# Hand-placed loads and casts for the first eight pairs of heads, decay terms stored in two parts, and a new spread of MLP groups over three batches

## The chip, the cores and the metric

The kernel runs on one core of one Trainium2 chip. The metric is device time in microseconds (us), lower is better. The kernel before was timed seven times; the median is 383.22 us.

## The reference, cut to what matters

There are 8 batches of 8 heads, 576 positions of 64 values each. Attention is causal and has a decay: with `cum` the running sum of `max(s, 0)` of a head, the score of query i and key j has `cum[j] - cum[i]` added. Its output, 4608 rows of 512 values (the heads of a batch side by side), goes through two layers with a hard-swish between them.

```python
scores = scale * q @ k.T + (cum[None, :] - cum[:, None])   # causal, cum = cumsum(max(s, 0))
attn   = exp(scores - max); attn = attn / sum(attn)
x      = attn @ v                     # -> (4608, 512), heads of a batch side by side
h      = x @ w_in                     # 512 -> 2048
out    = (h * clip(h + 3, 0, 6) / 6) @ w_out               # 2048 -> 512
```

## The kernel before, in words

**Heads go in pairs.** There are 32 pairs, four to a batch. For each pair, SP (the engine that only issues DMAs) loads q and k (`load_qk`, L136 to L144, two DMAs of 288 KB into `qkf`, three buffers) and v (`load_v`, L146 to L157, three DMAs into `v_f`, three slots). GpSimd (POOL) casts q and k to 16 bits (`cast_qk`, L165 to L168); v is cast on VectorE (DVE) for pairs 1 to 4 and on POOL otherwise (`cast_v`, L226 to L229). Slots of `v_f`, `v_h` and `qkT` are taken by pair number modulo 3, so a load into a slot waits until the pair three before it has given it back.

**Transposes.** For pairs 0 to 9, TensorE (PE) transposes the nine tiles of a pair in two groups of five and four (`transpose_group`, L242 to L256), and DVE copies each group into q and k rows of `qkT`, two copies per group. From pair 10 on, the DMA transposes (`transpose_dma`, L219).

**Decay.** The running sum, times 8, is split into three 16-bit terms (`kaug`, L110 to L117) and its negative into one (`qaug`, L460). They are extra rows 64 to 67 of the transposed k and q, beside rows of ones and rows of the coarse causal mask (`mask_rows`, L125), so that the scores' matmul adds them. Pair 0 gets its rows directly from SBUF, by four short DMAs on SP and four on ScalarE's queue (L461 to L468). For pairs 1 to 9, all 64 heads are first stored to a scratch in DRAM by two DMAs on SP (L469 and L472), and each pair loads its rows from there by two (`load_aug`, L159 to L163). From pair 10 on, `decay_columns` and `copy_columns` (L175 to L209) have made them columns of the block that the DMA transposes.

**Scores and attention.** A head's scores come in four banks (`scores_bank`, L272 to L319): one or two matmuls, an exponential on ScalarE (ACT), a triangular mask on POOL. `attend` (L320 to L350) multiplies by v with 15 matmuls; after the second head of a pair DVE takes the reciprocal of the row sums and multiplies. `x_transpose` (L356 to L377) turns the result into the input of the MLP, on PE (with a copy on DVE) or by DMA.

**MLP.** Nine blocks of 512 rows. A group of the first layer (`m1`, L403 to L420) is four matmuls, a relu on ACT and a gate on DVE; there are 16 to a block. A group of the second (`m2`, L421 to L445) is four matmuls, and four groups make one output tile of 128 rows, scaled on DVE and stored by SP. The two halves of w_in and the four quarters of w_out are loaded and cast by DMAs that POOL issues (`load_w_in`, `load_w_out`).

**Order.** Nothing is reordered by a scheduler: each engine runs its instructions in the order in which the program lists them, and waits where data or a buffer is missing.[...] `att_tasks` (from L482) lists the tasks of a pair: scores of the first head, the first transpose group of the *next* pair, the second attend of the *previous* pair, scores of the second head, casts for the next pairs, the second transpose group, `x_transpose` of the previous pair, then the first attend. Pairs 0 to 3 and the scores of pair 4 run alone. Then `weave` (L546) spreads the attention tasks of a batch evenly, by costs written beside each task, among the groups of the MLP: 24 groups with batch 1, 24 with batch 2, 32 with each of batches 3 to 7; 80 groups are left after the last pair.

PSUM tiles come from rings by tag: `M` (two, for layer 1 and early transposes), `S` (three, for scores, later transposes and the decay), `O` (one, of two banks), and `Y` (one, for layer 2).

Of the kernel before, what the change touches and what calls it, by code (L numbers as in the profile page):

```python
# [16 lines left out]
def kernel(  # L17
# [27 lines left out]
    PTD = 10  # L45
# [24 lines left out]
    )  # L70
    kaug_dram = nc.dram_tensor("kaug_scratch", (3, NH * SEQ), F16, kind="Internal").ap()
    qaug_dram = nc.dram_tensor("qaug_scratch", (1, NH * SEQ), F16, kind="Internal").ap()

# [34 lines left out]
    )  # L108
    kaug = work.tile([NH, 3, SEQ], F16, tag="s3", bufs=1)
    qaug = work.tile([NH, SEQ], F16, tag="s4", bufs=1)  # L110
    r1 = work.tile([NH, SEQ], F32, tag="s0", bufs=1)
# [6 lines left out]

    nc.gpsimd.memset(warm, 0.0)
    nc.gpsimd.memset(kT[:, :, W2:W2 + 64], 0.0)  # L120
# [14 lines left out]

    def load_qk(p, eng):  # L136
        b, h0 = (2 * p) // H, (2 * p) % H
        t = work.tile([128, NTR, 2, D], F32, tag="qkf", bufs=3, name=f"qkf{p}")
        for i, src in enumerate((q, k)):
            rows = src[b, h0:h0 + 2].rearrange("h s d -> (h s) d")  # L140
            eng.dma_start(
                out=t[:, :, i, :], in_=rows.rearrange("(t p) d -> p t d", p=128)
            )
        qk_f[p] = t  # L144
# [14 lines left out]
    def load_aug(p, eng):  # L159
        sl = p % NS  # L160
        c0 = p * W2
        eng.dma_start(out=kT[64:67, sl, 0:W2], in_=kaug_dram[:, c0:c0 + W2])
        eng.dma_start(out=qT[67:68, sl, 0:W2], in_=qaug_dram[:, c0:c0 + W2])  # L163

# [61 lines left out]
    def cast_v(p):  # L226
        sl = p % NS
        copy = nc.vector.tensor_copy if p in (1, 2, 3, 4) else nc.gpsimd.tensor_copy
        copy(out=v_h[:, sl, :, :, 0:D], in_=v_f[:, sl])  # L229
# [12 lines left out]
    def transpose_group(p, g):  # L242
        t0, t1 = ((0, 5), (5, 9))[g]
        n = (t1 - t0) * 128
        pT = half_bank(p < 5)
        src = qk_h[p]
        for t in range(t0, t1):
            c = (t - t0) * 128
            transpose_tile(pT[:, c:c + 128], src[:, t, :, :], t == t0, t == t1 - 1)
        sl = p % NS  # L250
        c0 = t0 * 128
        for dst, r0 in ((qT, 0), (kT, 64)):
            nc.vector.tensor_copy(out=dst[0:64, sl, c0:c0 + n], in_=pT[r0:r0 + 64, 0:n])  # L253
        if g == 1:
            qk_h.pop(p)
# [147 lines left out]
    def m1(n, f):  # L403
        if f == 0:
            gT[n] = work.tile([128, NF, 512], F16, tag="gT", bufs=2, name=f"gT{n}")
        ph = bank()
        for kc in range(KC):
# [13 lines left out]
    def m2(n, t4, part):  # L421
        if part == 0:

            if (n, t4) in ((0, 1), (8, 1), (8, 3)):
                pouts[n, t4] = bank()
            else:
                pouts[n, t4] = psum.tile([128, 512], F32, tag="Y", name=f"po{n}_{t4}")
# [27 lines left out]
    load_qk(0, nc.sync)  # L455
    load_v(0, nc.sync)
    load_qk(1, nc.sync)
# [7 lines left out]
    for hh in range(2):  # L465
        c0, c1 = hh * SEQ, (hh + 1) * SEQ
        nc.sync.dma_start(out=kT[65:66, 0, c0:c1], in_=kaug[hh:hh + 1, 1, :])
        nc.scalar.dma_start(out=kT[66:67, 0, c0:c1], in_=kaug[hh:hh + 1, 2, :])  # L468
    nc.sync.dma_start(  # L469
        out=kaug_dram.rearrange("r (h t) -> h r t", h=NH), in_=kaug  # L470
    )
    nc.sync.dma_start(out=qaug_dram.rearrange("r (h t) -> h (r t)", h=NH), in_=qaug)  # L472
    mask_rows(1, nc.scalar.copy)
    load_v(1, nc.sync)
    load_aug(1, nc.sync)
    load_qk(2, nc.sync)
    load_v(2, nc.sync)

    weights_at = {1: [(load_w_in, 0)], 2: [(load_w_in, 1)]}
    pairs_at = {0: [3], 1: [4], 2: [], 3: [5], 4: [6], 5: [7, 8]}  # L480

    def att_tasks(p):  # L482


        more = p + 1 < NP

        def loads():
            if p + 2 < PTD:
                load_aug(p + 2, nc.sync)
            if p == 5:  # L490
                load_columns()
            for m in pairs_at.get(p, [p + 3] if p + 3 < NP else []):
                load_qk(m, nc.sync)
                load_v(m, nc.sync)
            if 4 < p < PTD - 1:
                cast_qk(p + 1)

        def casts():
            if more:
                cast_v(p + 1)  # L500
            if p + 2 <= 4:
                cast_qk(p + 2)
            if PTD <= p + 2 < NP:
                cast_columns(p + 2)
                transpose_dma(p + 2)
            for load, c in weights_at.get(p, []):
                load(c)

        def scores(hd):
            return [(lambda bi=bi: scores_bank(hd, bi), 400) for bi in range(4)]  # L510

        tr = [[], []]
        if p + 1 < min(NP, PTD):
            tr = [[(lambda: transpose_group(p + 1, 0), 640)],
                  [(lambda: transpose_group(p + 1, 1), 512)]]
        here = tr if p != 4 else [[], []]
        late = [(lambda: attend(2 * p - 1), 1200)] if p > 0 else []
        back = [(lambda: x_transpose(p - 1), 0 if by_dma(p - 1) else 640)] if p > 0 else []
        a = [(loads, 0)]
        if p <= PXD:  # L520
            a += scores(2 * p) + here[0] + late
            a += scores(2 * p + 1) + [(casts, 0)] + here[1] + back
        else:
            s0, s1 = scores(2 * p), scores(2 * p + 1)
            a = late + (back + a if by_dma(p - 1) else a + s0[:2] + back)
            a += (s0 if by_dma(p - 1) else s0[2:]) + here[0]
            a += s1 + [(casts, 0)] + here[1]
        if p == 6:
            a += [(decay_columns, 640)]
        if p == 7:  # L530
            a += [(copy_columns, 0)]
        c = [(lambda: attend(2 * p), 1200)]
        if p == 4:
            c += [(lambda: cast_qk(p + 1), 0)] + tr[0] + tr[1]
        return a, c

    att_of = [[]]
    for p in range(NP):
        a, c = att_tasks(p)
        att_of[-1] += a  # L540
        if p % 4 == 0 and p > 0:
            att_of.append([])
# [28 lines left out]
    def merged(a, b, rounds):  # L571
# [10 lines left out]
        return out_  # L582

    keep_warm(18)
    cast_qk(0)
    transpose_group(0, 0)
    transpose_group(0, 1)
    mask_rows(2, nc.vector.tensor_copy)
    cast_v(0)
    cast_qk(1)  # L590
    keep_warm(12)
    for task, _ in att_of[0]:
        task()

    first = [(task, 0.0 if f < 4 else 0.7) for f, (task, _) in enumerate(m1_tasks(0))]
    for c, f in enumerate((0, 2, 5, 8)):
        task, w = first[f]
        first[f] = ((lambda task=task, c=c: (task(), load_w_out(c))), w)  # L600
    m2_0 = m2_tasks(0)
    weave(att_of[1], first + m2_0[:8])
    weave(att_of[2], merged(m1_tasks(1), m2_0[8:], 2))
    for n in range(2, NBLK):
        weave(
            att_of[n + 1] if n + 1 < B else [],
            merged(m1_tasks(n), m2_tasks(n - 1), 4),
            0.85 if n + 1 == B - 1 else 1.0,
        )
    for task, _ in m2_tasks(NBLK - 1):  # L610
        task()

# [29 lines left out]
```

## Time and profile before

| what | value |
|---|---|
| median of 7 runs | 383.22 us (378.83 to 384.9) |
| the profiled execution | 384.71 us |
| its span in the profile | 383.0 us |
| mean granted clock of PE | 0.966 |
| busy: PE, ACT, DVE, POOL | 358.2, 210.3, 190.6, 146.0 us |
| DMA | 59.38 MB, 155 GB/s over the span |

The profile divides the span into 40 slices. In the rows of section 2, each digit is the busy share of a slice in tenths, in the row PEclk the clock that PE was granted, in the row DMA the mean busy share of 16 DMA engines. A busy PE can be at half clock, so that the two rows belong together. The busy share of DMA can exceed one, as packets overlap. The lists of waits give what an engine waited for, and the chain of waits follows the end of the program back. Lines such as L408 are lines of the kernel before.

### The profile page before, as it was taken

The numbers are of one execution on the slowest core, as the hardware profiler recorded it, in microseconds if no ns is written. First come the engines' busy times: TensorE is split into PE (matmuls) and PEld (weight loads), VectorE is DVE, ScalarE is ACT, GpSimd is POOL, SyncE is SP. The second block draws the span as 40 slices with busy tenths as digits, with TensorE's granted clock in tenths as the row PEclk, the third lists the DMA queues.
The fourth block names the chain that finished last, engine by engine and source line by source line (L and its number), as shares of the span: only waits on it lengthen the run. The fifth ranks groups of instructions, "written<-read, shape, count | busy, mean of one in ns | idle before, by whom it ended". The sixth has DMA issues, their size and how long they took to land.

```text
span 383.0 us, 7609 instructions
## 1 busy us (share of the span) xinstructions
PE 358.2 (94%) x2780; PEld 222.5 (58%) x2780; DVE 190.6 (50%) x329; ACT 210.3 (55%) x406; POOL 146.0 (38%) x375
## 2 busy tenths in 40 slices
PE   7775886899999999999999999999999999999995
PEld 2464454556666666666666666666666655555542
DVE  5544476656545454544454445444544454454531
ACT  4735556334777666666666666666666533443310
POOL 4465353426555545355535554544443200000000
PEclk9969599889999999999999999999999999999999
DMA  8699799926899999999997999889944101001012
GB/s 175 137 202 197 162 216 213 209 59 149 175 224 189 219 207 193 232 190 203 219 227 160 206 200 231 181 190 225 187 109 107 47 27 56 27 39 45 27 61 78
DMA packets 184621, 59.38 MB, mean 155 GB/s; under 512 B 177828, under 2 KB 178212, under 8 KB 184584
## 3 DMA queue, kind: packets, MB, share of 16 engines
q1 hardware_dynamic: 182536, 54.52, 66.9%
q0 software_dynamic: 1632, 4.19, 5.8%
q8 instruction: 22, 0.36, 0.4%
q10 hardware_dynamic: 416, 0.19, 0.2%
q14 instruction: 15, 0.12, 0.1%
HBM read 37.41 MB, written 9.73 MB: 123 GB/s over the span
## 4 chain that ended last, share of the span: by engine, by line
PE 82%; DMA 9%; DVE 3%; ACT 2%; issue 1%; SPq 1%; POOL 1%; POOLq 0%; ACTq 0%; DVEq 0%
PE bank L408 31%; PE po L430 30%; PE S L282 10%; PE O L331 7%; DMA qkf<-in_k_dram 5%; DMA v_f<-in_v_dram 3%; PE bank L430 3%; ACT Pm L290 2%; DMA s_sb<-in_s_dram 1%; PE pT L369 1%; DVE qkT L253 1%; PE bank L450 1%; POOL t L167 1%; DVE kaug L115 0%; PE pT L238 0%
## 5 line engine op out<-in xcount | busy, mean ns | idle before, releaser
L416 ACT ACTIVATE trl<-bank,bias 128x512 f32<-128x512 f32 x144 | 99.4, 690 | 114.8 <-PE bank L408 113.8
L417 DVE SCALAR_TENSOR_TENSOR gT<-trl,bank 128x512 f16<-128x512 f32 x144 | 99.0, 687 | 123.3 <-ACT trl L416 123.3
L408 PE MATMUL bank<-xT,w_in 128*128 128x512 f16 x576 | 150.0, 387 | 0.6 <-DVE gT L417 0.6
L290 ACT ACTIVATE Pm<-S 128x384 f16<-128x384 f32 (+2 forms) x256 | 116.2, 505 | 34.1 <-PE S L282 32.6
L430 PE MATMUL po<-w_out_sb,gT 128*128 128x512 f16 x528 | 131.8, 381 | 0.0
L295 POOL TENSOR_SCALAR_AFFINE_SELECT Pm<-Pm 128x128 f16<-128x128 f16 (+2 forms) x256 | 78.6, 310 | 138.6 <-ACT Pm L290 129.5
L408 PEld LDWEIGHTS <-w_in 128*128 128x128 f16 x576 | 77.7, 146 | 32.1 <-issue 3.7
L430 PEld LDWEIGHTS <-gT 128*128 128x128 f16 x576 | 53.4, 98 | 51.7 <-issue 0.5
L282 PE MATMUL S<-qkT 128*128 128x320 f16 (+4 forms) x448 | 71.4, 269 | 6.0 <-DMA qkT<-kaug_scratch 2.4
L282 PEld LDWEIGHTS <-qkT 128*128 128x128 f16 x448 | 42.2, 101 | 34.6 <-DMA qkT<-kaug_scratch 2.5
L331 PEld LDWEIGHTS <-Pm 128*128 128x128 f16 x960 | 40.2, 100 | 11.8 <-POOL Pm L295 0.4
L331 PE MATMUL O<-v_h,Pm 128*128 128x65 f16 x960 | 42.8, 197 | 0.2 <-POOL Pm L295 0.2
L343 DVE TENSOR_TENSOR xs<-O,r 128x640 f16<-128x640 f32 x32 | 26.4, 824 | 1.1
L213 POOL CAST xb<-qkf 128x1152 f16<-128x1152 f32 x22 | 25.2, 1147 | 0.0
L439 DVE TENSOR_SCALAR osb<-po 128x512 f32<-128x512 f32 x33 | 22.6, 684 | 5.0 <-PE po L430 5.0
L229 POOL CAST v_h<-v_f 128x640 f16<-128x640 f32 x28 | 20.6, 736 | 2.8 <-DVE gT L417 2.8
L341 DVE RECIPROCAL r<-O 128x10 f32<-128x10 f32 x32 | 7.0, 220 | 25.7 <-PE O L331 25.5
L167 POOL CAST t<-qkf 128x1152 f16<-128x1152 f32 x10 | 11.9, 1187 | 13.6 <-DMA qkf<-in_k_dram 13.6
L238 PEld LDWEIGHTS <-t 128*128 128x128 f16 x90 | 6.6, 101 | 13.9 <-POOL t L167 9.9
L253 DVE COPY qkT<-pTm 64x640 f16<-64x640 f16 (+1 forms) x20 | 9.1, 454 | 8.3 <-PE pTm L238 8.0
L253 DVE COPY qkT<-pT 64x640 f16<-64x640 f16 (+1 forms) x20 | 9.0, 452 | 6.1 <-PE pT L238 6.0
L430 PE MATMUL bank<-w_out_sb,gT 128*128 128x512 f16 x48 | 11.3, 379 | 0.0
(40 smaller groups left out, 80.5 us busy)
## 6 DMA issues: line engine op xcount, KB each, us to landing
qkf<-in_q_dram SPq DMA_DIRECT2D x32, 288.0 KB, 3.6
qkf<-in_k_dram SPq DMA_DIRECT2D x32, 288.0 KB, 4.3
out_dram<-osb SPq DMA_DIRECT2D x36, 256.0 KB, 2.0
v_f<-in_v_dram SPq DMA_DIRECT2D x64, 128.0 KB, 3.9
w_in<-in_moe_w_in_dram POOLq DMA_DIRECT2D x2, 1024.0 KB, 11.7
w_out_sb<-in_moe_w_out_dram POOLq DMA_DIRECT2D x4, 512.0 KB, 8.4
v_f<-in_v_dram SPq DMA_DIRECT2D x32, 32.0 KB, 7.4
qkT<-xb SPq DMA_TRANSPOSE x22, 5.0
```

The lines of the kernel that those rows point to most:

```text
L213: nc.gpsimd.tensor_copy(out=x.rearrange("p (i t) c -> p t i c", i=2)[:, :, :, 0:D], in_=qk_f.pop(p))
L253: nc.vector.tensor_copy(out=dst[0:64, sl, c0:c0 + n], in_=pT[r0:r0 + 64, 0:n])
L282: nc.tensor.matmul(out=S[:, c:c + hi - lo], lhsT=kT[:, sl, off + 128 * kt:off + 128 * (kt + 1)], rhs=qT[:, sl, off + lo:off + hi], start=( ...
L290: nc.scalar.activation(out=P[:, p0:p0 + n], in_=S[:, 0:n], func=AF.Exp, scale=0.125, bias=0.0)
L295: nc.gpsimd.affine_select(out=view, in_=view, pattern=pattern, compare_op=ALU.is_ge, fill=0.0, base=0, channel_multiplier=-1,)
L331: nc.tensor.matmul(out=O[:, hh, qt * VW:qt * VW + D + 1], lhsT=P[:, c:c + 128], rhs=v_h[:, sl, hh, kt, 0:D + 1], start=(qt == 0), stop=(qt ...
L343: nc.vector.tensor_tensor(out=xs.rearrange("p t h d -> p h t d"), in0=Ov[:, :, :, 0:D], in1=r.to_broadcast([128, 2, 5, D]), op=ALU.mult,)
L408: nc.tensor.matmul(out=ph, lhsT=w_in_t[f // 8][:, kc, f % 8, :], rhs=xT[:, kc, n * 512:(n + 1) * 512], start=(kc == 0), stop=(kc == KC - 1),)
L416: nc.scalar.activation(out=trl, in_=ph, func=AF.Relu, bias=bias3[:, 0:1], scale=1.0)
L417: nc.vector.scalar_tensor_tensor(out=gT[n][:, f, :], in0=trl, scalar=6.0, in1=ph, op0=ALU.min, op1=ALU.mult)
L430: nc.tensor.matmul(out=po, lhsT=gT[n][:, f, t4 * 128:(t4 + 1) * 128], rhs=w_out_sb[:, f, :], start=(f == 0), stop=(f == NF - 1),)
L439: nc.vector.tensor_scalar_mul(out=osb, in0=po, scalar1=1.0 / 6.0)
```

## The change

The decay terms are built in one tile `aug` of four q rows and four k rows per head, the ones included (POOL sets them). Heads 0 to 7 are stored by one DMA on ACT's queue, followed there by the load of pair 1's rows; heads 8 to 19 are stored later by SP; the other heads are not stored. Each pair loads its rows by one DMA.

Three lists replace the one for pairs 0 to 7: `first_tasks` for pairs 0 to 3, `block0_tasks` for pairs 4 to 7, with loads, casts and weight loads written out; `att_tasks` starts at pair 8. In `block0_tasks` a pair's transposes, scores, both attends and `x_transpose` follow each other within the pair. All 32 groups of MLP block 0 run with batch 1, 24 groups with each of batches 2 and 3, 32 with each of 4 to 7, and 80 at the end as before. Every third group of layer 1 of block 0 takes the `Y` bank, and two more output tiles take `M`. `cast_v` of pair 0 moves to DVE, of pair 4 to POOL.

```diff
+    NA = 8
+    aug_drams = [
+        nc.dram_tensor("aug_scratch0", (2, 4, NA * SEQ), F16, kind="Internal").ap(),
+        nc.dram_tensor("aug_scratch1", (2, 4, (2 * PTD - NA) * SEQ), F16, kind="Internal").ap(),
+    ]
...
+    nc.gpsimd.memset(aug[:, 0, 0:3, :], 1.0)
+    nc.gpsimd.memset(aug[:, 1, 3, :], 1.0)
...
-        copy = nc.vector.tensor_copy if p in (1, 2, 3, 4) else nc.gpsimd.tensor_copy
+        copy = nc.vector.tensor_copy if p < 4 else nc.gpsimd.tensor_copy
...
-        pT = half_bank(p < 5)
+        pT = half_bank(p < 4)
...
-        ph = bank()
+        if n == 0 and f % 3 == 2:
+            ph = psum.tile([128, 512], F32, tag="Y", name="bankY")
+        else:
+            ph = bank()
...
     load_qk(0, nc.sync)
-    load_v(0, nc.sync)
     load_qk(1, nc.sync)
...
-    nc.sync.dma_start(
-        out=kaug_dram.rearrange("r (h t) -> h r t", h=NH), in_=kaug
-    )
-    nc.sync.dma_start(out=qaug_dram.rearrange("r (h t) -> h (r t)", h=NH), in_=qaug)
-    mask_rows(1, nc.scalar.copy)
-    load_v(1, nc.sync)
-    load_aug(1, nc.sync)
+    load_v(0, nc.sync)
     load_qk(2, nc.sync)
-    load_v(2, nc.sync)
...
+    def first_tasks(p):
+        def loads():
+            if p == 0:
+                load_qk(3, nc.sync)
+                load_v(2, nc.sync)
+                store_aug(1, NA, 2 * PTD, nc.sync)
+            elif p == 1:
+                load_aug(2, nc.sync)
+                load_aug(3, nc.sync)
+                load_v(3, nc.sync)
+            else:
+                load_pair(p + 2)
+        def casts():
+            cast_v(p)
+            if p < 2:
+                cast_qk(p + 2)
+            if p == 1:
+                load_w_in(0)
...
+    def block0_tasks(p):
+        def ahead():
+            load_pair(p + 3)
+            cast_qk(p + 1)
+            cast_v(p + 1)
+            if p == 4:
+                for c in range(4):
+                    load_w_out(c)
+            if p == 5:
+                load_columns()
+        return (
+            [(lambda: transpose_group(p, 0), 640), (lambda: transpose_group(p, 1), 512)]
+            + scores(2 * p)
+            + scores(2 * p + 1)
+            + [(ahead, 0), (lambda: attend(2 * p), 1200), (lambda: attend(2 * p + 1), 1200)]
+            + [(lambda: x_transpose(p), 640)]
+            + ([(lambda: transpose_group(8, 0), 640), (lambda: transpose_group(8, 1), 512)]
+               if p == 7 else [])
+        )
...
     transpose_group(0, 1)
-    mask_rows(2, nc.vector.tensor_copy)
-    cast_v(0)
+    mask_rows(1, nc.vector.tensor_copy)
+    store_aug(0, 0, NA, nc.scalar)
+    load_aug(1, nc.scalar)
+    load_v(1, nc.sync)
     cast_qk(1)
     keep_warm(12)
-    for task, _ in att_of[0]:
-        task()
+    for p in range(4):
+        run(first_tasks(p))
+    load_pair(6)
+    cast_qk(4)
+    cast_v(4)
+    load_w_in(1)
+    keep_warm(4)
+    attend(7)
+    x_transpose(3)
...
-    weave(att_of[1], first + m2_0[:8])
-    weave(att_of[2], merged(m1_tasks(1), m2_0[8:], 2))
+    run(m1_0[:3])
+    weave(block0_tasks(4), m1_0[3:10])
+    weave(block0_tasks(5), m1_0[10:])
+    run(m2_0[:2])
+    weave(
+        block0_tasks(6) + [(decay_columns, 640), (copy_columns, 0)] + block0_tasks(7),
+        m2_0[2:],
+        0.85,
+    )
+    m2_1 = m2_tasks(1)
+    weave(att_of[0], m1_tasks(1) + m2_1[:8])
+    weave(att_of[1], merged(m1_tasks(2), m2_1[8:], 2))
```

## The prediction

> **What bounds the kernel now.** I read the busy tenths of the page first, then what TensorE waits for up to 110 us and after it, then the chain of waits, then the timelines of the queues up to 110 us.
>
> ```profile
> PE   7775886899999999999999999999999999999995
> PEclk9969599889999999999999999999999999999999
> DMA  8699799926899999999997999889944101001012
> ```
>
> A slice is 9.6 us. TensorE is full from the twelfth slice on, at full clock; of its waits from 110 us on the list is empty. All that can be won lies in the first 107 us. In them TensorE has this to do, by the instructions counted in the windows and the pitch of each in undisturbed stretches of its timeline: 150 layer matmuls in fours of 0.86 us are 32.3; 22.3 heads of scores at 0.69 are 15.4; 20.7 attends at 0.47 are 9.7; ten pairs of transposes at 0.5 are 5; ten transposes of x at 0.3 are 3; the decay transposes 1.6. Together 67 us: 40 are lost. The first layer group begins at 43.3, with 14.5 us done: 28.8 are lost before it, and 11.2 from there to 107.
>
> TensorE's waits up to 110 us (line, total, times, longest), two of fourteen:
>
> ```profile
> PE pTm L238 <- POOL t L167: 4.8, 2, 3.6
> ...
> PE S L282 <- DMA qkT<-kaug_scratch: 2.4, 1, 2.4
> ```
>
> The first is the cast of pair 2, whose loads SP issues only at 15.65, behind the store of all decay terms and the loads of v. The chain shows what holds the second and a later one (start, us, what):
>
> ```profile
> 27.62 12.06 DMA v_f<-in_v_dram
> ...
> 51.35 14.20 DMA qkf<-in_k_dram
> ```
>
> Loads that land within 2.6 to 4.6 us elsewhere take 12 and 14 here. The queues say beside what (packets, MB, share of 16 engines), and the issues give the weights' landing:
>
> ```profile
> q1 hardware_dynamic: 182536, 54.52, 66.9%
> q0 software_dynamic: 1632, 4.19, 5.8%
> ```
> ```profile
> w_in<-in_moe_w_in_dram POOLq DMA_DIRECT2D x2, 1024.0 KB, 11.7
> w_out_sb<-in_moe_w_out_dram POOLq DMA_DIRECT2D x4, 512.0 KB, 8.4
> ```
>
> **What the Trainium skill says.** *DMA: Bandwidth & Descriptors*, Queues, rings and completion order: an engine round-robins between queue rows "at packet granularity". The trace agrees: a weight packet is 2.6 KB, one of SP's 0.3 KB, and the small ones starve. The weights' 22 us of DMA time (5.8% of 383) make each half of w_in 5.5, 0.47 of the DMA over 11.7 us. SP's loads keep about 0.55 beside one half in flight, and 0.2 beside two (26.6 to 43). The same page, Two DMAs through the same engine are not ordered: who reads what a DMA wrote must wait for its semaphore. Here the kaug store lands 2.2 us after its issue, the qaug store 2.6. *TensorE: Matmul & The Clock Gate*, The HAM clock gate: clock at half after an idle window of some 3.4 us. The windows agree: 0.50 at 20 to 26 us and 38 to 46, after 3.5 us idle and after 2.4 plus 1.1. The same page, Architectural detail: the array is 16× 32×32, calls the queues of ScalarE and VectorE strict FIFO; the timelines show each in program order.
>
> **The change, part by part.**
>
> *Start.* qk1 moves ahead of v0 and no longer waits for a landed v load (k1 issued at 3.4, not 7.7). The two stores of all 64 heads (288 KB) leave SP; eight heads go from ScalarE's queue (72 KB), twelve more from SP later (108 KB); each later pair has one decay load for two. On SP, four short loads of pair 0 end near 9.5, v0 waits for landings on reused semaphores (issues 11.0 to 13.3), qk2 goes at 13.3 and 13.9 and lands at 18.0 (k took 4.1 before), not 20.2. POOL's new memsets (2304 columns at 0.53 us per 512, 2.4 us) fit before 7.4, when its first cast starts. The new wait: store at 10.55 on ScalarE, landed at 13.2, load to 13.9; the exponentials queued behind it start at 13.9, not 13.27. That 0.6 us dies in the wait for pair 2 (the round trip on this queue is unmeasured: at the 4.4 us of the identity's load it would be 2 us more, of which some 0.8 shows; below the 2.2 of the kaug store I exclude): transposes at 19.4 instead of 21.55, and with 1.1 us idle instead of 3.5 the clock drop goes. From a pair's first transpose to the next pair's 3.4 to 4.4 us pass at full clock (27.22 to 31.72 before). So: scores of pair 2 at 22.8, pair 3 at 27.3, last attend of pair 3 at 32.7, normalize 1.1, transpose 0.3 and copy 0.5: 34.7. w_in's first half is issued behind the cast of pair 3, at 23.7, and lands at 35.2 (11.3 to 12.0). **First layer group at 35.2**, with 12.6 us done (four pairs of 3.15): 22.6 lost, 6.2 fewer than before.
>
> *Weights.* v4 needs 5.4 us of DMA from 24 on at 0.55: 33.8. Its cast holds POOL; w_in's second half goes at 34.6 and lands at 46.3, before layer group 8 needs it (35.2 + 10.9 plus clock). The four of w_out go behind the casts of pair 5, at 48.8, and need 11 us at 0.94: 61, against a need at 68. Both hidden, the latter by seven us; uncovered they cost their delay one for one.
>
> *Pairs 4 to 7 with all of block 0.* Work: 32 groups, 27.6; scores 5.5, attends 3.8, transposes of x 1.1, of pairs 4 to 8 2.5, decay 1.5: 42.0. But transposes, scores, both attends and the transpose of x of one pair now stand close together, where before a pair's second attend and its x came a pair later. I walked TensorE's, ScalarE's and VectorE's orders with 0.86, 0.69 (relu), 0.69 (gate), 0.41 (exponential at pitch), 0.5 (one copy), 1.04 (reciprocal and product). Waits in us: pair 4's scores on copies behind four gates, 1.6; x of pair 4 behind a gate and the product, 1.35; pair 5's scores 2.0 (the gate ahead ends 1.45 after its matmuls, two copies 1.0, against 0.5 of transposes); second attend of pair 5 0.8, its x 0.7; pair 6's scores 0.85; smaller ones 1.3. Last the decay:
>
> ```profile
> 75.44 1.14 PE L192 MATMUL pD<-ident,kaug 64*128 64x64 f16 x20 [1.37 <-DVE qkT L253]
> ```
> ```profile
> 77.19 1.68 DVE L205 COPY dec<-pD 128x128 f16<-128x128 f16 x8
> ```
> ```profile
> 86.52 1.84 DVE L177 COPY xb<-xaug 128x1152 f16<-128x1152 f16 x2
> ```
>
> Decay copies (75.8 to 78.9, 3.1) and xb's two (1.84) were a pair apart; now both stand ahead of pair 7's copies (1.0): 5.9 on VectorE, covered by one layer group, transposes and part of the decay matmuls: 3.3 stay. Sum of waits 11.9. Clock: half speed costs up to 1.7 us per window, likely at 35.2 (2.2 idle in 2.5) and after the decay: 2.8 of 3.4. A third bank for block 0's groups removes the bank wait (0.63 at 48.35), nothing more. End of block 0: 35.2 + 42.0 + 11.9 + 2.8 = **91.9**, with 54.6 done. Before reaches 54.6 at 107 - 12.4 = 94.6. **Gain 2.7.**
>
> *Batches 2 and 3* now carry 24 groups each, later ones 32; in all the work is the same. A pair then has 7.9 us, while its DMA time is 9.4 (mean share 1.05 over 110 to 200 us, a pair per 9.6 us, less half an output). That needs a share of 1.18; eight us at 124 reached 1.20. Loads run over two pairs ahead; I take 0.6 lost, bounds 0 and 7.5. No gain can come here, TensorE being full.
>
> Sum: -6.2 + (11.9 + 2.8 - 11.2) + 0.6 = **-2.1**. The profiled execution took 384.71 (span 383.0 and 1.7 around it), 1.5 above the median of seven, 383.22. So 382.6 for it, **381.1** at the median.
>
> **Rivals.**
> 1. *The short pipeline costs little.* If only the decay and pair 5's wait stay (5.3) and the clock holds, block 0 ends at 82.5: -12.1, 371; half of that, 375, is my figure. For: three layer banks, and at 55 to 64 us layers and attention interleave with no idle time of TensorE. Against: the order, where scores follow their own transposes directly.
> 2. *DMA becomes the bound in batches 2 and 3 (slower).* If it cannot exceed 1.05, eight pairs take 71.5 us, not 64: +7.5, **388.6**. It undoes the gain from a ceiling of about 1.14. For: a mean of 1.05 in a stretch of steady work. Against: there loads land in 3.1 to 4.3 us, so it isn't full.
> 3. *The loads move, the time doesn't.* If v4 again lands 12.1 after its issue (25.5), w_in's second half lands at 51 and group 8 waits 3.2, with a clock drop 1.7: 386.
>
> **How the numbers follow.** A measurement of this kernel can tell about 1%, 379.4 to 387.1, from no change. Likeliest (chance 0.45): 381.1, own range 377 to 386 (clock 0 to 5, waits 9 to 15). Rival 1 0.27, rival 2 0.18, rival 3 0.10. The range 371 to 389 takes in rival 1 to its end and rival 2 to just above its worked price. Faster by over 1%: rival 1 and a quarter of the likeliest, 0.38. Slower by over 1%: most of rival 2, a third of rival 3, 0.20. Between: 0.42.
>
> **What would show it.** Right: pair 2's transposes near 19.4 at full clock; first layer group near 35; no wait of layer groups on weights; waits of scores on VectorE's copies at pairs 5 and 7 of about 2 and 3 us; block 0 done near 92. Wrong: layers waiting for w_in or w_out, the first exponential later than 15, waits of TensorE after 110, or gaps in pairs 4 to 7 under 6 us together.

## The result, and the profile after

| | before | after |
|---|---|---|
| median | 382.94 us (378.83 to 385.44, 62 runs) | 385.38 us (383.88 to 387.5, 25 runs) |
| ratio after / before | | 1.0083, 95% interval 1.0065 to 1.0102 |
| profiled execution, its span | 384.71, 383.0 us | 385.74, 384.0 us |
| mean granted clock of PE | 0.966 | 0.996 |

The change made the kernel slower: by 0.8% in the ratio, by 2.4 us between the medians. The ratio leaves out the slow executions, those over 1.5% above the fastest of their kernel (nine of before's 62, the profiled one among them), and the medians do not, so that it is not their quotient. The forecast was 381.1. The profiled execution of before was itself 1.8 us above its median.

The same three rows of the page, for the kernel after (slices of 9.6 us):

```profile
PE   7768868879999899999989999999999999999995
...
PEclk9989999999999999999999999999999999999999
DMA  9699989952699999998999999999944101001012
```

The clock row has lost its fives, as forecast, but a second execution of before (below) has none either. The row of PE was nine from the twelfth slice to the last but one; it now has an eight at the fourteenth slice (125 to 134 us) and at the twenty-first (192 to 202 us).

TensorE's waits from 37 us (the first layer group is at 37.45) to 93 us, then from 110 us to the end (line, releaser, total, times, longest; for before the second list was empty):

```profile
PE S L291 <- DVE qkT L262: 5.4, 4, 1.9
PE pT L378 <- DVE xs L352: 3.7, 5, 1.2
PE S L291 <- ACT Pm L299: 0.9, 2, 0.4
PE pT L247 <- DVE dec L216: 0.7, 1, 0.7
PE O L340 <- POOL Pm L304: 0.2, 1, 0.2
```
```profile
PE S L291 <- DMA qkT<-xb: 3.5, 3, 1.5
PE O L340 <- POOL Pm L304: 0.5, 2, 0.2
```

The first list is the short pipeline of pairs 4 to 7: scores that wait for the copies of their own transposes, and transposes of x that wait for the product just before. The second is new: scores wait for blocks that the DMA transposes, at 132 us (1.45, pair 13), at 149 (0.69) and at 194 (1.33). The first two stand in batch 3, the last in batch 4, which has 32 groups:

```profile
193.60 0.34 PE L291 MATMUL S<-qkT 128*128 128x256 f16 x2 [1.33 <-DMA qkT<-xb]
```

**Lost time by stage.** Waits in the list leave out stalls between matmuls that are too short to be listed. So I count, for every stretch, the matmuls that TensorE did in it and price them nearly as the prediction did (0.2158 us a layer matmul, so 0.863 a group; scores 0.69 a head, attends 0.47, transposes 0.5 a pair, x 0.3; for the decay 0.8, half of what the prediction gave it, once in every row; warm-up nothing). Elapsed time less that work is lost time. One stretch, batch 3 of after, 128.3 to 163.5 us, by groups of instructions:

```profile
L420 PE MATMUL bank<-xT,w_in 128*128 128x512 f16 x65 | 16.9, 383 | 0.0
L442 PE MATMUL po<-w_out_sb,gT 128*128 128x512 f16 x36 | 9.2, 379 | 0.0
L291 PE MATMUL S<-qkT 128*128 128x320 f16 (+4 forms) x56 | 8.2, 262 | 2.1 <-DMA qkT<-xb 2.1
L340 PE MATMUL O<-v_h,Pm 128*128 128x65 f16 x141 | 6.4, 193 | 0.2 <-POOL Pm L304 0.2
```

101 layer matmuls are 21.8 us, 8 heads of scores (56 matmuls) 5.5, 9.4 attends 4.4, five transposes 0.3: 32.0 of 35.2. Lost: 3.2, of which 2.3 stand in the column of idle time. In steady batches the account closes: from 200 to 300 us every kernel below is within 0.4 us of nothing lost. Lost us by stage (the columns end at fixed times, so work moves a little between them; sums count). Behind 40 us the account was taken in stretches of 20 us; a matmul on an edge counts in both, so that the last column comes out some 1.0 to 1.7 low. In one piece before loses 1.2 there and after 6.8; the difference is nearly the same. The edits are explained in the next section:

| kernel | 0 to 40 | 40 to 100 | 100 to 200 | ratio to before |
|---|---|---|---|---|
| before, as shown | 26.6 | 16.2 | 0.2 | 1 |
| before, profiled again | 25.4 | 13.0 | -0.2 | |
| after | 24.9 | 13.0 | 5.3 | 1.0083 |
| v loads on POOL | 23.8 | 13.4 | 4.1 | 1.0054 |
| fewer bytes | 24.1 | 13.5 | 3.6 | 1.0027 |
| the spread of before | 23.6 | 17.8 | 3.1 | 1.0138 |
| x behind the next transposes | 24.0 | 10.3 | 4.8 | 0.9976 |
| decay behind pair 7's scores | 23.4 | 12.1 | 4.8 | 1.0039 |
| casts between the scores | 24.1 | 13.5 | 4.4 | 1.0089 |
| pair 2's decay load first | 23.1 | 14.5 | 4.4 | 1.0089 |
| layer 1 of block 1 spaced out | 24.3 | 13.1 | 4.7 | 1.0045 |
| both edits of block 0 | 23.4 | 9.5 | 4.3 | 0.9933 |
| both, spread 24, 28, 28 | 23.8 | 13.8 | 1.6 | 1.0008 |
| both, v loads on POOL | 26.0 | 8.9 | 2.1 | 0.9900 |

Against before profiled again, after wins 0.5 us up to 40, nothing up to 100, and loses 5.5 from 100 to 200: 5.0 in all, where the two profiled executions differ by 385.74 - 380.83 = 4.9.

How far one execution can be trusted, the table shows too. From after on, all rows but that of pair 2's decay load run the same program up to the first layer group, and yet this group starts anywhere from 35.85 to 38.64 us (median 36.46; the execution of after shown here has 37.45). Four kernels whose program from 100 to 200 us is that of after (x, decay, pair 2's decay load, both edits) lose 4.3 to 4.8 there, after itself 5.3. A difference of this size between two rows shows nothing.

### The profile page after: what moved, and what is told of

Same layout as the page of the kernel before. It is cut to its first block, busy times and chain, and to the rows that moved or that the text cites. A ratio compares the mean times of both kernels' runs of the same rounds, so it can differ in the third digit from the quotient of the medians.

```text
span 384.0 us, 7603 instructions
## 1 busy us (share of the span) xinstructions
PE 354.9 (92%) x2784; PEld 218.9 (57%) x2784; DVE 190.2 (50%) x331; ACT 207.4 (54%) x404; POOL 147.7 (38%) x377
## 4 chain that ended last, share of the span: by engine, by line
PE 77%; DMA 9%; DVE 6%; ACT 2%; SPq 2%; issue 1%; POOL 1%; ACTq 0%; POOLq 0%
PE bank L420 28%; PE po L442 27%; PE S L291 10%; PE O L340 6%; DMA qkT<-xb 6%; PE bank L442 3%; ACT Pm L299 2%; DVE xs L352 1%; DMA qkf<-in_k_dram 1%; PE bankY L420 1%; DVE qkT L262 1%; PE pT L378 1%; DMA qkT<-aug_scratch 1%; SPq L157 1%; DMA s_sb<-in_s_dram 1%
## 5 line engine op out<-in xcount | busy, mean ns | idle before, releaser
L428 ACT ACTIVATE trl<-bank,bias 128x512 f32<-128x512 f32 x139 | 96.2, 692 | 108.2 <-PE bank L420 107.2
L429 DVE SCALAR_TENSOR_TENSOR gT<-trl,bank 128x512 f16<-128x512 f32 x139 | 95.5, 687 | 117.0 <-ACT trl L428 116.7
L420 PE MATMUL bank<-xT,w_in 128*128 128x512 f16 x556 | 142.6, 382 | 0.0
L442 PE MATMUL po<-w_out_sb,gT 128*128 128x512 f16 x496 | 122.9, 379 | 0.0
L291 PE MATMUL S<-qkT 128*128 128x320 f16 (+4 forms) x448 | 69.8, 263 | 13.8 <-DVE qkT L262 5.4
L442 PEld LDWEIGHTS <-gT 128*128 128x128 f16 x576 | 53.2, 98 | 50.8
L291 PEld LDWEIGHTS <-qkT 128*128 128x128 f16 x448 | 40.8, 98 | 42.3 <-DVE qkT L262 6.4
L340 PEld LDWEIGHTS <-Pm 128*128 128x128 f16 x960 | 39.0, 98 | 13.7 <-POOL Pm L304 1.6
L442 PE MATMUL bank<-w_out_sb,gT 128*128 128x512 f16 x80 | 19.4, 379 | 0.0
L262 DVE COPY qkT<-pT 64x640 f16<-64x640 f16 (+1 forms) x24 | 10.9, 453 | 3.3 <-PE pT L247 3.0
L462 PE MATMUL bank<-warm 128*128 128x512 f16 x34 | 10.1, 459 | 2.2 <-POOL warm L116 1.4
L262 DVE COPY qkT<-pTm 64x640 f16<-64x640 f16 (+1 forms) x16 | 7.3, 454 | 8.4 <-PE pTm L247 8.1
```

The lines of the kernel that those rows point to most:

```text
L291: nc.tensor.matmul(out=S[:, c:c + hi - lo], lhsT=kT[:, sl, off + 128 * kt:off + 128 * (kt + 1)], rhs=qT[:, sl, off + lo:off + hi], start=( ...
L340: nc.tensor.matmul(out=O[:, hh, qt * VW:qt * VW + D + 1], lhsT=P[:, c:c + 128], rhs=v_h[:, sl, hh, kt, 0:D + 1], start=(qt == 0), stop=(qt ...
L420: nc.tensor.matmul(out=ph, lhsT=w_in_t[f // 8][:, kc, f % 8, :], rhs=xT[:, kc, n * 512:(n + 1) * 512], start=(kc == 0), stop=(kc == KC - 1),)
L428: nc.scalar.activation(out=trl, in_=ph, func=AF.Relu, bias=bias3[:, 0:1], scale=1.0)
L429: nc.vector.scalar_tensor_tensor(out=gT[n][:, f, :], in0=trl, scalar=6.0, in1=ph, op0=ALU.min, op1=ALU.mult)
L442: nc.tensor.matmul(out=po, lhsT=gT[n][:, f, t4 * 128:(t4 + 1) * 128], rhs=w_out_sb[:, f, :], start=(f == 0), stop=(f == NF - 1),)
```

## The experiments

Theories: **P**, the order within block 0 (each step directly behind the one it depends on) eats what the start wins; **Q**, batches 2 and 3 lose because six groups to a pair are too short for loads, casts and transposes by DMA, be it by bytes, by SP's issues or by latency; **R**, the profiled execution of before was not a typical one, and part of the forecast gain was chance in it. All ratios are to before, timed in the same series on the same chip, with a 95% interval behind them. The change itself was timed only in its own series (1.0083), not beside the kernels below, so a difference of some 0.003 from it is not resolved.

**Before, profiled again.** No edit.

> The kernel before, unchanged, profiled once more, because its shown execution lies 1.8 us above its own median at a mean clock of 0.966. If that execution carried a chance loss of clock, this one shows a span near 381 with fewer half-clock stretches before 107 us; if not, a span near 383 and the same clock.

Its span was 379.1 us, below what was expected, and it took 380.83, 3.9 less than the execution shown and 1.1 less than the median of its series (381.90). The first layer group came at 39.87 and not 43.30. Its clock row:

```profile
PEclk9989899899999999999999999999999999999999
```

The fives are gone: 38 to 46 us had a clock of 0.50 in the first execution and 0.79 in this. Up to the first layer group the clock is at half for 13.7 us in the first execution and for 5.2 in this; half of the difference, 4.3 us, is more than enough for the 3.4 (an estimate, as not all of that time was work). R holds: 3.4 us of the start that the forecast counted as lost by the order of loads came and went with the execution.

**v loads of pairs 11 to 18 issued by POOL.**

```diff
-                load_v(p + 3, nc.sync)
+                load_v(p + 3, nc.gpsimd if p + 3 < 19 else nc.sync)
```

> The v loads of pairs 11 to 18 are issued by GpSimd instead of SP: the same bytes, three DMAs fewer per pair on SP (about 2.3 of its 8.1 us). Theory A, SP's issue time binds batches 2 and 3: the waits of scores for the DMA transposes (3.5 us) go, time 2 to 3.5 us below the changed kernel, about equal to before. Theory B, the DMA engines are at their ceiling: the waits stay within 1 us, and so does the time.

1.0054 (1.0031 to 1.0077), which overlaps the interval of the change. Waits for transposed blocks after 93 us: 2.1, none over 0.8. But of after's 3.5, too, 2.1 stand in batches 2 and 3, and from 100 to 160 us this kernel loses 4.6, after 4.3. So in the batches that it was meant for the traces show no gain. SP itself gained little: with some 2.3 us of issues per pair gone, its transposes from 100 to 123 us come 7.3 to 7.7 us apart instead of 8.1, as their own issues take 3.5 to 4.0 us, not 2.7 to 3.0. So the 8.1 us are not a fixed need.

**Fewer bytes, as many DMAs.** The two larger v loads of pairs 11 to 18 fetch one of four tiles; the kernel leaves the rest of v out and uses old values in its place.

```diff
+            n = 1 if 11 <= p < 19 else 4
...
-                out=v_f[:, sl, hh, 0:4, :],
-                in_=v[b, h0 + hh, 0:512].rearrange("(t p) d -> p t d", p=128),
+                out=v_f[:, sl, hh, 0:n, :],
+                in_=v[b, h0 + hh, 0:128 * n].rearrange("(t p) d -> p t d", p=128),
```

> The two larger v loads of pairs 11 to 18 fetch one tile of four (that part of v is left out, old values are used): 192 KB of 864 less per pair, the same number of DMAs in the same order on SP. Theory A, SP's issue time: waits for the DMA transposes stay at 2.5 us or more, time within 1 us of the changed kernel. Theory B, DMA ceiling: the waits go, 2 to 3.5 us faster.

1.0027 (1.0005 to 1.0048), below the interval of the change; waits 1.8. From 100 to 160 us it loses 3.9, after 4.3; most of what its trace gains on after is the stretch from 180 to 200 us, where after waits for a block at 194. So neither theory came true: the time falls, the loss of the batches stays. From 108 to 148 us the mean share of DMA is 0.97 here and 1.10 in after, and the loss is nearly the same: bytes do not set it. Nor is there a fixed ceiling of 1.05 (rival 2): from 116 to 156 us the mean share is 1.11 in after and 1.15 with v on POOL. A higher ceiling is not excluded.

**The spread of before** (24, 24, 32), with all else as after, but that two output tiles go back from `M` to `Y`.

```diff
-        m2_0[2:],
+        m2_0[2:8],
...
-    weave(att_of[0], m1_tasks(1) + m2_1[:8])
-    weave(att_of[1], merged(m1_tasks(2), m2_1[8:], 2))
-    for n in range(3, NBLK):
+    weave(att_of[0], merged(m1_tasks(1), m2_0[8:], 2))
+    for n in range(2, NBLK):
```

> Only the spread is undone: 24, 24 and 32 groups with batches 1, 2 and 3 as before, everything else as in the changed kernel. If batches 2 and 3 lose what the start and block 0 had won (2.1 by pace, 3.5 by waits, less what before lost there): no waits for DMA transposes, 3 to 5 us below the changed kernel, 380.5 to 382.5, faster than before by up to 0.6%. If the loss comes from block 0's own order: within 1 us of the changed kernel.

1.0138 (1.0086 to 1.0191, six executions): not faster, and perhaps slower still, as the interval overlaps that of the change. The first forecast failed. The account suggests why: it loses 3.1 from 100 to 200 instead of 5.3, but 17.8 from 40 to 100 instead of 13.0, as the groups that it takes from batch 1 are missing beside block 0's waits. The waits for transposed blocks did not go, either: 0.58 us at 112 and 1.33 at 120, in batch 2, where before has none with the same 24 groups. So the number of groups is not all: batch 2 also holds the scores of pair 8 here, which before ran with batch 1, and what block 0 leaves behind on the queues may differ. The runs do not separate these.

**x behind the next pair's transposes**, in block 0 alone.

```diff
+        x_of = [(lambda: x_transpose(p - 1), 640)] if p > 4 else []
         return (
             [(lambda: transpose_group(p, 0), 640), (lambda: transpose_group(p, 1), 512)]
+            + x_of
...
-            + [(lambda: x_transpose(p), 640)]
-            + ([(lambda: transpose_group(8, 0), 640), (lambda: transpose_group(8, 1), 512)]
+            + ([(lambda: transpose_group(8, 0), 640), (lambda: transpose_group(8, 1), 512),
+                (lambda: x_transpose(p), 640)]
```

For p = 7 its own x comes behind the transposes of pair 8.

> In block 0, the transpose of a pair's x is put behind the next pair's transposes instead of ahead of them; nothing else changes. After the change, TensorE waits between 37 and 93 us 3.7 us for x (product on VectorE) and 5.4 us for the copies of transposed q and k. Short-pipeline theory (block 0 loses what it does because each step directly follows the one it depends on): most of the 3.7 us goes, and part of the 5.4, since 0.3 us of x transposes and a layer group come between copies and scores; block 0 is 3 to 6 us shorter, ratio to before 0.993 to 1.001. Rival (another engine's pace, or loads, set block 0's length): the waits only move to another instruction, block 0's length within 1 us of 55.0, ratio 1.006 to 1.010.

0.9976 (0.9956 to 0.9996): 1.07% better than the change, by moving four transposes. Block 0, from its first layer group to the first of block 1, takes 51.6 us, not 55.0. TensorE's waits from 36 to 93 us in this kernel, the three largest of seven:

```profile
PE S L291 <- DVE qkT L262: 1.8, 2, 1.0
PE S L291 <- ACT Pm L299: 1.7, 4, 0.6
PE pT L378 <- DVE xs L352: 1.2, 1, 1.2
```

How it works is seen at pair 5 on TensorE's timeline (start, us, instruction, idle time before it), first in after, then here:

```profile
52.29 0.45 PE L378 MATMUL pT<-ident,xs 128*128 128x128 f16 x5 [1.14 <-DVE xs L352]
52.58 1.03 PE L420 MATMUL bank<-xT,w_in 128*128 128x512 f16 x4
53.45 0.67 PE L247 MATMUL pT<-ident,t 128*128 128x128 f16 x9
56.01 0.34 PE L291 MATMUL S<-qkT 128*128 128x256 f16 x2 [1.90 <-DVE qkT L262]
```
```profile
50.64 0.67 PE L247 MATMUL pT<-ident,t 128*128 128x128 f16 x9
51.14 0.44 PE L378 MATMUL pT<-ident,xs 128*128 128x128 f16 x5
51.42 1.04 PE L420 MATMUL bankY<-xT,w_in 128*128 128x512 f16 x4
53.20 0.34 PE L291 MATMUL S<-qkT 128*128 128x256 f16 x2 [0.75 <-DVE qkT L262]
```

In after, x waits 1.14 for its product, and the transposes that need nothing stand in line behind it; their copies start that much later and the scores wait 1.90. Turned round, the nine transposes cover the product, and x and a layer group cover most of the copies: 3.04 us of waits become 0.75. P holds. A new wait of 0.5 us, on w_out, shows that the last weights are no longer quite hidden.

**Decay behind pair 7's scores.**

```diff
-        block0_tasks(6) + [(decay_columns, 640), (copy_columns, 0)] + block0_tasks(7),
+        block0_tasks(6)[:-1] + [(copy_columns, 0)] + block0_tasks(6)[-1:]
+        + block0_tasks(7)[:10] + [(decay_columns, 640)] + block0_tasks(7)[10:],
```

> The decay transposes and their copies stand behind pair 7's transposes and scores, and the copies of the mask columns ahead of pair 6's x, where after the change both stood directly ahead of pair 7's copies. The forecast put 3.3 us on that place; the trace of after shows 0.72 plus 1.62 us there. If the queue of copies on VectorE is the cause, both waits go and block 0 is 1.5 to 2.3 us shorter, ratio 1.002 to 1.005. If VectorE is merely busy in this stretch, the waits turn up at pair 7's x or at pair 8, and the ratio stays 1.007 to 1.010.

1.0039 (1.0018 to 1.006). The wait for `dec` is gone from the list and that for copies falls from 5.4 to 4.1. Block 0 is 1.0 us shorter (54.0), less than the 1.5 to 2.3 expected; of the 3.0 us between the two spans another 1.6 are in the start, which is chance.

**Casts and transpose of the pair two ahead between the two heads' scores**, from pair 9 on.

```diff
-            a += (s0 if by_dma(p - 1) else s0[2:]) + tr[0]
-            a += s1 + [(casts, 0)] + tr[1]
+            a += (s0 if by_dma(p - 1) else s0[2:]) + [(casts, 0)] + tr[0]
+            a += s1 + tr[1]
```

> From pair 9 on, the casts and the DMA transpose of the pair two ahead are placed between the two heads' scores instead of behind the second head's, so they start about 3 us earlier; no byte, DMA or instruction is added. Latency theory (at 6 groups to a pair, the 6 us landing of a transpose plus the queue on SP no longer fits into the time from its cast to the scores): the 3.5 us of waits of scores for transposed blocks after 110 us vanish, ratio 1.000 to 1.003. DMA-ceiling theory (rival 2 of the forecast): bytes set the pace, waits stay at 2 to 3.5 us, ratio 1.006 to 1.010. SP-issue theory: SP's issues have no gap from 101 to 151 us, so starting the casts earlier doesn't start the transposes earlier, and the waits stay too, with the transposes still 8.1 us apart.

1.0089 (1.0064 to 1.0115), no gain, though the waits named are gone. What TensorE waits for after 93 us in this kernel:

```profile
PE O L340 <- POOL Pm L304: 1.9, 6, 0.4
```

All 3.5 us of waits for transposed blocks went, and 100 to 200 us still loses 4.4, not 5.3. The casts now stand ahead of the second head's masks on POOL, and attends wait for those six times. Only 1.9 of the 4.4 are waits in the list. So the late transpose is where the loss shows, not a cause that stands alone. My reading, not shown: POOL, SP and DMA are all tight at this pace, and what one is relieved of shows at the next. My expectation, that the wait is the loss, was wrong.

**Pair 2's decay load first on SP.**

```diff
             if p == 0:
                 load_qk(3, nc.sync)
-                load_v(2, nc.sync)
-                store_aug(1, NA, 2 * PTD, nc.sync)
             elif p == 1:
                 load_aug(2, nc.sync)
+                load_v(2, nc.sync)
                 load_aug(3, nc.sync)
                 load_v(3, nc.sync)
+                store_aug(1, NA, 2 * PTD, nc.sync)
```

> On SP, pair 2's load of decay rows is issued ahead of the v loads of pair 2 and of the store for heads 8 to 19, instead of behind them; same DMAs. In after, SP issued it at 22.2 us and the scores of pair 2 waited 1.84 us for it. If SP's order there cost the start its gain, that wait goes, the first layer group starts at 35.5 to 36.3 instead of 37.5 and the ratio is 1.003 to 1.005. If the transposes or the cast of pair 3 are late in any case, the first layer group stays within 0.5 us of 37.5.

1.0089 (1.0059 to 1.012). The wait of 1.84 is gone and the first layer group starts at 35.56:

```profile
35.56 1.95 PE L420 MATMUL bank<-xT,w_in 128*128 128x512 f16 x8 [0.99 <-DMA w_in<-in_moe_w_in_dram]
```

It waits for the first half of w_in, and 1.0 us more goes later on the second half. The start is 1.9 us earlier than in the execution of after shown, but only 0.9 earlier than the median of the executions with the same start (36.46), and 1.0 us is lost again to the second half of w_in: the time does not move. The forecast for the start came true, the one for the ratio did not.

**Layer 1 of block 1 spaced out** in batch 2.

```diff
-    m2_1 = m2_tasks(1)
-    weave(att_of[0], m1_tasks(1) + m2_1[:8])
+    m1_1, m2_1 = m1_tasks(1), m2_tasks(1)
+    weave(
+        att_of[0],
+        m1_1[:6] + m2_1[:1] + m1_1[6:10] + m2_1[1:2] + m1_1[10:14] + m2_1[2:3]
+        + m1_1[14:] + m2_1[3:8],
+    )
```

> The change with one edit in batch 2: the first four groups of layer 2 of block 1 stand among its 16 layer-1 groups instead of behind them, so that a pair carries some 4.8 relus, not 6, beside its eight exponentials. From 100 to 120 us the change loses 1.7 us (elapsed less counted work), before 0.8, both with few waits listed. If ScalarE's pace is the cause, 0.7 to 1.5 us come back: ratio 1.004 to 1.007. If not (short pairs, or transposes by DMA that land late), the stretch still loses 1.5 or more and the ratio stays at 1.007 to 1.010.

1.0045 (1.0026 to 1.0065), but the stretch from 100 to 120 us loses 1.4, not 1.7, and 100 to 200 loses 4.7. The ratio is what ScalarE's pace would give, the stretch is not: x and decay, which change nothing there, lose 1.2 and 1.4 in it. I leave this one open.

**Both edits of block 0.** The decay transposes stand behind all eight score banks of pair 7, as in the run with that edit alone; the "first seven" of the expectation is a miscount. The copies of the mask columns now come ahead of pair 6's second attend, as its x has moved.

> Both edits of block 0 together: x behind the next pair's transposes, and the decay transposes behind pair 7's first seven score banks. Alone they gave 0.9976 and 1.0039 against 1.0083 for the change. If block 0's waits are two separate faults, the gains add: 0.9976 - 0.0044 = 0.993, interval 0.991 to 0.996, first layer group of block 1 near 86.5 us. If both took the same waits away (pair 7's), the ratio stays at 0.997 or above.

0.9933 (0.9903 to 0.9963). The gains add as two separate faults would. Block 0 says the same, with the start taken out: 55.0 us in after, 51.6 with x moved, 54.0 with decay moved, 50.8 with both; the first layer group of block 1 comes at 86.67.

**Both, and 24, 28, 28 groups over batches 1 to 3**, so that a pair of batches 2 and 3 has seven. Two output tiles go back from `M` to `Y`, and the groups of the two layers alternate in batch 2, where in after all of layer 1 comes first.

```diff
-        m2_0[2:],
+        m2_0[2:8],
...
-    weave(att_of[0], m1_tasks(1) + m2_1[:8])
-    weave(att_of[1], merged(m1_tasks(2), m2_1[8:], 2))
+    weave(att_of[0], merged(m1_tasks(1), m2_0[8:], 2) + m2_1[:4])
+    weave(att_of[1], merged(m1_tasks(2), m2_1[4:12], 2) + m2_1[12:])
```

> The two edits of block 0 as in the kernel of the two together, and the spread 24, 28, 28 groups over batches 1 to 3 instead of 32, 24, 24: a pair of batches 2 and 3 has 7 groups, one of batch 1 six. Short-pair theory (six groups give a pair 7.9 us, less than its casts, its transposes by DMA and the issues on SP need): from 100 to 160 us the change loses 4.3 us and this 1 or less; but block 0's pairs have less to hide behind and lose up to 3 more; ratio 0.989 to 0.994 against 0.993 for the two edits alone. If the losses of batches 2 and 3 come from somewhere else (order on SP after block 0, or ScalarE), they stay above 3 us and the ratio is above 0.994.

1.0008 (0.9988 to 1.0029). After 93 us TensorE waits for no transposed block any more; all that is listed is

```profile
PE po L442 <- DVE osb L451: 1.0, 2, 0.5
```

and 100 to 200 us loses 1.6, not 4.3 (100 to 160: 1.9, where 1 or less was expected, against 4.6). Q holds in that more groups to a pair take most of the loss away. That the groups alternate has a part in it that this run does not separate; spacing them alone, above, left 4.7. But block 0's pairs, with six groups each, lose 13.8 instead of 9.5. I had allowed 3 us for that; it is 4.3, and the trade comes out worse.

**Both, and the v loads of pairs 11 to 18 on POOL.**

> The two edits of block 0, and the v loads of pairs 11 to 18 issued by GpSimd. On the change alone that move took the ratio from 1.0083 to 1.0054. If SP's issues are a cause of what batches 2 and 3 lose, it adds: 0.003 below the two edits together, near 0.990, and the waits for transposed blocks after 93 us fall from 2.6 to 1 us or less. If what it gains on SP it loses on GpSimd's casts and masks, it equals the two edits together within 0.002.

0.9900 (0.9863 to 0.9938), 378.09 us against 382.14: the fastest of all, about 1% under before. The loss from 100 to 200 falls from 4.3 to 2.1, and the waits for transposed blocks from 2.2 to 0.9. Its interval overlaps that of the two edits alone, so that what POOL adds rests on the traces, one of each kernel. On the change alone the same move showed nothing from 100 to 160 us, so I call its effect likely, not shown.

## Why the prediction was wrong, point by point

**The base.** "So 382.6 for it, 381.1 at the median" carried the profiled execution's clock drops into the gain. The first layer group at 43.3 was 3.4 us later than in a second execution of the same kernel (39.87). That execution lies 1.1 under the median of its series, so at the median some 2 to 3 us of the forecast -6.2 were never there to win (an estimate from these starts). The first step that failed is the subtraction of 22.6 from 28.8.

A second error of the base hid behind it. "150 layer matmuls", "22.3 heads", "20.7 attends" and "ten transposes of x" count too much: in one window from 0 to 107 us the trace has 143, 21.9, 20.0 and 8. At the prediction's own prices the work is 64.3 us, not 67, and 42.7 are lost, not 40: 13.9 behind the first layer group instead of 11.2. So block 0 had some 2.7 us more to win than the sum has, and the sum would have been near -4.8.

The clock was misread as well. "After 3.5 us idle and after 2.4 plus 1.1" does not fit the trace: the clock fell at 19.4 and at 36.4 us, 1.4 and 1.1 us after these two waits of 3.56 and 2.38 had begun, and the wait of 1.1, from 40.0, found it at 0.50 already.

**The start.** "First layer group at 35.2" came at 37.45, in a late execution; the median of all with this start is 36.46. Pair 2's transposes came at 20.04 at full clock (forecast 19.4), its scores at 25.55, not 22.8, and behind them the granted clock was 0.50 from 26.5 to 29.9 us. I had counted the stores that left SP, and not the place of the new decay load in SP's queue: it is issued at 22.17, behind v loads and a store, and costs 1.84 us (0.7 to 2.6 in the other executions):

```profile
22.17 0.99 SPq L169 DMA_DIRECT2D qkT<-aug_scratch  x2
```
```profile
25.55 0.72 PE L291 MATMUL S<-qkT 128*128 128x256 f16 x6 [1.84 <-DMA qkT<-aug_scratch]
```

The load of w_in that the forecast had at 35.2 was right, as the start with that wait removed shows (35.56). That the first weights are hidden held only because the start was late, which is luck.

**Weights.** In after no layer group waits for them. Right. That the small packets starve beside the large ones, from which their landing was worked out, no run tested.

**Pairs 4 to 7 with block 0.** Forecast 91.9, measured 92.46. Waits forecast 11.9, listed 9.7 from the first layer group on; the largest at the places named (scores of pair 5 2.0, measured 1.90; pair 7 3.3 with the decay, measured 0.72 + 1.62). The clock loss of 2.8 did not come. With 42.0 of work the 9.7 make 51.7, and block 0 took 55.0: another 3.3 us are stalls too short for the list, for which the forecast had no term. So the places of the waits were right, and the end of block 0 came out right by luck: a start 2.3 late, a clock that did not drop, stalls not counted. Rival 1 had the waits wrong: the order costs nearly what I walked out, and turning it round gives 3.4 us of it back.

**Batches 2 and 3.** "I take 0.6 lost, bounds 0 and 7.5" is the term that failed and turned the sign. From 100 to 200 us 5.3 are lost, where before loses 0.2; 4.3 of them lie before 160 us, in batches 2 and 3. The bound of 7.5 held, the value in it did not. I argued from bytes, that "loads run over two pairs ahead". What the runs put in its place is the length of a pair: with seven groups instead of six the loss falls from 4.3 to 1.6. How a short pair meets a chain, SP's queue in after shows (the transposes of pairs 12 and 13, with all that SP issues between):

```profile
117.97 3.00 SPq L229 DMA_TRANSPOSE qkT<-xb  x1
121.07 1.24 SPq L370 DMA_TRANSPOSE xT<-xs  x1
122.36 0.58 SPq L148 DMA_DIRECT2D qkf<-in_q_dram  x1
122.98 0.59 SPq L148 DMA_DIRECT2D qkf<-in_k_dram  x1
123.62 1.70 SPq L157 DMA_DIRECT2D v_f<-in_v_dram  x2
125.36 0.62 SPq L161 DMA_DIRECT2D v_f<-in_v_dram  x1
126.09 2.79 SPq L229 DMA_TRANSPOSE qkT<-xb  x1
```
```profile
132.19 0.56 PE L291 MATMUL S<-qkT 128*128 128x256 f16 x4 [1.45 <-DMA qkT<-xb]
```

There is no gap: SP issues for 8.1 us a pair here, and a pair of six groups has 7.9 on TensorE (the prediction's count). The cast that the second transpose needs ended at 123.2, so the transpose leaves 2.9 late, lands at 132.2, and the scores that could have started at 130.7 wait. But this wait alone is not the loss: with the casts earlier all such waits went and 4.4 us stayed. From 100 to 160 us after loses 4.3, the kernel with fewer bytes 3.9, the one with v loads on POOL 4.6; with both edits of block 0 in place the same move goes with 3.0 instead of 4.6. Only more groups to a pair took most of it away. Which of SP, POOL and DMA is the first limit at this pace stays open.

**Rivals.** Rival 2 had the right place and sign, and the wrong mechanism: a ceiling of 1.05 is passed, and with a share of 0.97 the loss stays. Its sign, waits of TensorE after 110 us, came. Rival 3 did not occur.

## What to carry to other kernels

When the bound engine is full in steady state, moving its work forward to hide a start has to be paid for where it is taken from: work out the length of the shortest period that remains, and hold it against what each queue (its issues, too) needs for one period. Where no margin is left, allow for a loss; here none of the queues alone was shown to be its cause. In a hand-written order, put a step that depends on nothing new between each step and the one that consumes it; here the order of two neighbours was worth 1.07%. Profile the baseline twice before costing a gap in it. And count work in one window: sums over many windows count what lies on their edges twice.

## What the runs showed of the hardware that was not expected

The granted clock of TensorE differs between executions of one and the same kernel: 0.966 and 0.986 on average, 0.50 and 0.79 from 38 to 46 us, with 3.4 us between the starts of the first layer group.

Its drops come in steps. Read in windows of half a us, every drop to half clock up to 120 us, in all fourteen executions, lasts 3.4, 6.8 or 10.2 us: one, two or three steps of 3.41. Within one execution the starts lie whole steps apart: 19.36, 36.43, 67.15 and 77.39 in the execution of before shown (5, 9 and 3 steps), 21.03, 38.10 and 65.41 in the other (5 and 8). So the steps have the same length but start elsewhere in each execution.

The length of a wait alone does not tell whether the clock drops. In after it drops at 26.5 us, behind a wait of 1.84 us; with x moved, the same place of the same program has a wait of 1.76 and no drop, with v loads on POOL one of 1.11 and a drop. From 38 to 100 us after has waits of 1.0 to 1.9 and a clock of 1.00. That it is the place of a wait among the steps that decides would fit this, but is not shown.

A transpose by DMA of a pair's q and k in after takes SP 2.7 to 4.2 us to issue, and lands 5.0 to 6.1 us after it; with the v loads gone from SP the issues from 100 to 123 us take 3.5 to 4.0.
